# Three F blocks instead of two per step in the six-expert part of an attention and mixture-of-experts kernel: 15 block products for 18, sums kept in PSUM, prepared weights kept in DRAM

## The chip, the cores and the metric

The kernel runs on one core of one Trainium2 chip. The metric is the device time of one execution in microseconds (us), the median of several runs. Engines are named as in the profile: PE is the matrix engine (PEld its weight loads), DVE the vector engine, ACT the scalar engine, POOL the GpSimd engine, SP the engine that issues nearly all DMAs.

## The reference, cut to what matters

An attention-like recurrence over 768 positions (4 batches, 8 heads, head size 48) gives x, a matrix of N = 3072 tokens by D = 384. A mixture of experts follows:

```python
N, D, E, F = (3072, 384, 8, 1024)
logits = x @ w_gate
logits = logits - logits.max()
P = np.exp(logits)
for _ in range(8):
    P /= P.sum(1, keepdims=True) + 1e-09
    P /= P.sum(0, keepdims=True) + 1e-09
    P *= N / E
out = np.zeros((N, D), dtype=np.float32)
for e in range(E):
    h = np.maximum(x @ w1[e], 0.0)
    ye = h @ w2[e]
    out += P[:, e:e + 1] * ye
```

Every expert sees every token. Arithmetic is kept near fp32 by splitting each operand into a rounded high part and a low rest (`fp32r` tiles); a product is three matmuls, high by high, high by low, low by high.

## The kernel before

Three stages follow each other on PE. In phase 1 (`phase1`) the recurrence runs sub-block by sub-block of 256 tokens, and experts 0 and 1 run right behind it on the same tokens (`experts`); x is written to DRAM (`x_d`) and so are the two experts' results (`ye_d`). Phase 2a (`phase2a`) finishes experts 0 and 1 for the last sub-block, does the first three of the eight normalising rounds (`rows`, `columns`) and prepares the first tokens and weights. Phase 2b (`phase2b`) is the six-expert part: experts 2 to 7 for all tokens, and the other five rounds in its first steps.

The six-expert part takes the tokens in units of 768, each as two halves of 384 (`TH`), and F in blocks of 128. The first layer of one step multiplies 2 blocks of F (rows of a small block matrix A) by 3 blocks of D by the 2 token halves (blocks B11 to B32), which would be 12 block products of 128 x 128 by 128 x 384. It does them in 11, over sums of weight blocks (S1 to S5) and of token blocks (T1 to T4), in seven calls of `prod` (P1 to P7, four of them with two block products). Each `prod` fills a PSUM bank of its own from the pool `psA` of two; DVE and ACT combine them in SBUF tiles (`u2`, `u3`, `c11`, ...). `relu` makes the split activations `hh` and `hl` of each (F block, token half): one ACT and one DVE instruction.

The second layer of a step runs one step later: `second(st, k)` adds into the accumulator `po[k]`, one of six (3 token tiles by 2 halves, each a PSUM bank), 2 F blocks by 3 matmuls. `l2(k)` puts one such call behind each product, so PE alternates between the layers. There are 96 steps: 2 passes of tokens (`SU`), 6 experts, 2 units, 4 pairs of F blocks.

`prep_w` makes the weights of one pair: five sums on DVE, then four split pairs, the high part by ACT, the low part by DVE. It runs 48 times, since each pass prepares all weights anew from the raw weights, which `raw_w` loads. `load_x` makes the nine token blocks of a unit. When an expert is done, each accumulator is scaled by P and added to the output tile `oa` by DVE (L863).

PE runs in the order in which the program is written (`manual_schedule`). The instructions of ACT, DVE, POOL and SP are put in order by a scheduler, which moves weight and token preparation ahead to where it expects its data; each engine then runs its queue strictly in that order.

## Time and profile before

| what | value |
|---|---|
| runs | 1823.38, 1823.28, 1821.69 us; median 1823.28 us |
| profiled execution, span first to last instruction | 1819.5 us (3.8 us less than the median of the runs, which also hold what lies around the span) |
| mean granted TensorE clock | 0.997 |
| PE, PEld, DVE, ACT, POOL busy | 97%, 95%, 75%, 40%, 5% of the span |
| six-expert part, first to last matmul's start | 639.95 to 1813.26 us |
| bytes moved by DMA | 132.86 MB, 73 GB/s in the mean |

No time of the profiled execution itself is given beside its span. A busy PE is not a PE at its peak: a matmul of 384 columns has a duration of 335 ns in the profile, but matmuls overlap, and the distance between the starts of two is what counts. DVE instructions that follow each other without a wait overlap a little too. Rows in groups show the mean duration of one instruction in ns behind the total in us.

### The profile page before, as it was taken

The numbers are of one execution on the slowest core, as the hardware profiler recorded it, in microseconds if no ns is written. First come the engines' busy times: TensorE is split into PE (matmuls) and PEld (weight loads), VectorE is DVE, ScalarE is ACT, GpSimd is POOL, SyncE is SP. The second block draws the span as 40 slices with busy tenths as digits, with TensorE's granted clock in tenths as the row PEclk, the third lists the DMA queues.
The fourth block names the chain that finished last, engine by engine and source line by source line (L and its number), as shares of the span: only waits on it lengthen the run. The fifth ranks groups of instructions, "written<-read, shape, count | busy, mean of one in ns | idle before, by whom it ended". The sixth has DMA issues, their size and how long they took to land.

```text
span 1819.5 us, 30778 instructions
## 1 busy us (share of the span) xinstructions
PE 1768.3 (97%) x12062; PEld 1726.9 (95%) x12062; DVE 1360.0 (75%) x3038; ACT 730.1 (40%) x1607; POOL 89.4 (5%) x168
## 2 busy tenths in 40 slices
PE   6999899999999999999999999999999999999998
PEld 4888899999999989999999999998999999999998
DVE  8898999898863778867675767587776767675754
ACT  7544444454543533334242434243433334342421
POOL 3100211111110000000000000000000000000000
PEclk9999999999999999999999999999999999999999
DMA  7433534443422421301020101232220101020100
GB/s 223 120 101 103 134 107 123 128 111 98 117 80 91 137 81 53 122 18 53 1 70 1 59 12 53 71 105 68 88 70 18 53 18 53 2 69 1 53 27 29
DMA packets 104506, 132.86 MB, mean 73 GB/s; under 512 B 9632, under 2 KB 82080, under 8 KB 104352
## 3 DMA queue, kind: packets, MB, share of 16 engines
q1 hardware_dynamic: 98944, 120.89, 21.9%
q0 software_dynamic: 4608, 9.52, 2.1%
q8 instruction: 97, 1.59, 0.4%
q14 instruction: 57, 0.47, 0.1%
q10 hardware_dynamic: 800, 0.39, 0.1%
HBM read 88.22 MB, written 23.59 MB: 61 GB/s over the span
## 4 chain that ended last, share of the span: by engine, by line
PE 81%; DVE 11%; DMA 3%; ACT 2%; issue 1%; SPq 1%; DVEq 0%; ACTq 0%
PE po L856 10%; PE po L854 10%; PE po L855 10%; PE P L893 9%; PE P L894 9%; PE P L895 9%; PE ph L222 9%; PE po L195 3%; PE po L197 3%; PE po L196 3%; PE sp L561 2%; PE y L578 2%; DMA raw<-in_w_dram 1%; PE U L554 1%; DVE c L903 1%
## 5 line engine op out<-in xcount | busy, mean ns | idle before, releaser
L856 PE MATMUL po<-wc,hl 128*128 128x384 f32 x1152 | 385.9, 335 | 3.2 <-DVE hl L915 3.2
L854 PE MATMUL po<-wc,hh 128*128 128x384 f32 x1152 | 385.5, 335 | 0.1
L855 PE MATMUL po<-wc,hh 128*128 128x384 f32 x1152 | 385.4, 335 | 0.0
L914 ACT ACTIVATE hh<-c 128x384 fp32r<-128x384 f32 x384 | 200.9, 524 | 324.6 <-DVE c L903 323.1
L915 DVE SCALAR_TENSOR_TENSOR hl<-c,hh 128x384 fp32r<-128x384 f32 x384 | 212.8, 555 | 66.5 <-ACT hh L914 58.5
L222 PE MATMUL ph<-xh,w 128*128 128x256 f32 x1152 | 225.9, 281 | 2.1 <-ACT xh L630 1.2
L856 PEld LDWEIGHTS po<-wc,hl 128*128 128x128 f32 x1152 | 216.5, 188 | 4.7 <-DVE hl L915 4.7
L854 PEld LDWEIGHTS po<-wc,hh 128*128 128x128 f32 x1152 | 216.4, 188 | 0.4 <-ACT hh L914 0.4
L855 PEld LDWEIGHTS po<-wc,hh 128*128 128x128 f32 x1152 | 216.5, 188 | 0.0
L908 ACT ACTIVATE s<-P 128x384 f32<-128x384 f32 x192 | 94.1, 490 | 273.3 <-PE P L895 273.2
L222 PEld LDWEIGHTS ph<-xh,w 128*128 128x128 f32 x1152 | 185.5, 189 | 3.1 <-ACT xh L630 1.8
L234 ACT ACTIVATE hh<-ph 128x256 fp32r<-128x256 f32 x192 | 73.3, 382 | 223.5 <-PE ph L222 223.1
L893 PE MATMUL P<-B,wa 128*128 128x384 f32 x480 | 160.9, 335 | 0.9 <-DVE c L903 0.7
L895 PE MATMUL P<-B,wa 128*128 128x384 f32 x480 | 160.6, 335 | 0.0
L894 PE MATMUL P<-B,wa 128*128 128x384 f32 x480 | 160.6, 335 | 0.0
L222 PE MATMUL ph<-xl,w 128*128 128x256 f32 x576 | 153.9, 282 | 2.0 <-DVE xl L631 2.0
L195 PE MATMUL po<-w,hh 128*128 128x384 f32 x384 | 140.6, 366 | 0.6 <-ACT yst L200 0.5
L197 PE MATMUL po<-w,hl 128*128 128x384 f32 x384 | 130.1, 339 | 2.6 <-DVE hl L236 2.6
L903 DVE TENSOR_TENSOR c<-P,u 128x384 f32<-128x384 f32 x192 | 106.7, 556 | 31.0 <-PE P L895 29.6
L903 DVE TENSOR_TENSOR u<-u,s 128x384 f32<-128x384 f32 x96 | 53.5, 558 | 101.8 <-ACT s L908 101.7
L196 PE MATMUL po<-w,hh 128*128 128x384 f32 x384 | 129.4, 337 | 0.0
L236 DVE TENSOR_TENSOR hl<-hf,hh 128x256 fp32r<-128x256 f32 x192 | 80.4, 421 | 45.9 <-ACT hf L235 43.8
(175 smaller groups left out, 3516.6 us busy)
## 6 DMA issues: line engine op xcount, KB each, us to landing
raw<-in_w_dram SPq DMA_DIRECT2D x48, 768.0 KB, 4.3
qs<-z POOLq DMA_DIRECT2D x144, 64.5 KB, 3.7
qk<-in_aqk_dram SPq DMA_DIRECT2D x12, 768.0 KB, 6.0
ks<-kh SPq DMA_DIRECT2D x144, 64.0 KB, 3.1
ye_d<-yst SPq DMA_DIRECT2D x48, 192.0 KB, 2.1
y<-ye_d SPq DMA_DIRECT2D x48, 192.0 KB, 2.4
z<-in_aqk_dram SPq DMA_DIRECT2D x11, 768.0 KB, 5.6
B<-x_d SPq DMA_DIRECT2D x40, 192.0 KB, 4.0
```

The costliest lines, as they stand in the source:

```text
L195: nc.tensor.matmul(po[k], hh[:, s], w2h, start=f == 0, stop=False)
L196: nc.tensor.matmul(po[k], hh[:, s], w2l, start=False, stop=False)
L197: nc.tensor.matmul(po[k], hl[:, s], w2h, start=False, stop=f == NF - 1)
L222: nc.tensor.matmul(ph, w[:, k, ct * 128:ct * 128 + 128], x[:, ct, :], start=q == 0, stop=q == len(terms) - 1)
L854: nc.tensor.matmul(po[k], hh[:, s], w2[:, 0, i], start=first, stop=False)
L855: nc.tensor.matmul(po[k], hh[:, s], w2[:, 1, i], start=False, stop=False)
L856: nc.tensor.matmul(po[k], hl[:, s], w2[:, 0, i], start=False, stop=last)
L893: nc.tensor.matmul(ps, t[:, 0, k], x[:, 0], start=first, stop=False)
L894: nc.tensor.matmul(ps, t[:, 0, k], x[:, 1], start=False, stop=False)
L895: nc.tensor.matmul(ps, t[:, 1, k], x[:, 0], start=False, stop=last)
L914: A.activation(hh, c, AF.Relu)
L915: V.scalar_tensor_tensor(hl, c, 0.0, hh.bitcast(F32), ALU.max, ALU.subtract)
```

## The change

One step now takes three blocks of F: 3 rows of A by 3 blocks of D by 2 token halves, 18 block products done in 15 (P1 to P15, each one block product of three matmuls). There are 64 steps: 4 units, 16 sets of three F blocks (`NT`; a set may span two experts). One unit is now one pass over all weights; odd units go through the sets backwards.

- **Sums in PSUM.** The products run in a fixed order over two banks (`psX`): X and P use bank a, Y, Z and V bank b. A bank is read by ACT or DVE after a product, and the next product adds into the same bank, so the matmul has to wait until that reader is done. DVE does 10 additions and 6 `hl` a step, ACT 5 copies and 6 `hh`.
- **Second layer.** `order` lists 18 units (6 accumulators by 3 F blocks, three matmuls each); `fill(k)` puts k of them behind a product. At the start of a pass 8 (`FRONT`) come first.
- **Weights.** `prep_w` makes a set once, in the first unit: 12 sums on POOL (3 of 256 columns, 9 of 128), then six split pairs on ACT and DVE into four ring tiles (wa, wb, wc, wd), each stored to DRAM (`wd`). Units 1 to 3 load them with `load_set`, four DMAs of 768 KB a step. The raw weights of a set are one tile of 1152 KB, and there is one such buffer, so the load of the next set waits until POOL, ACT and DVE have read this one. The ring has 10 tiles (12 before).
- **Tokens.** All 15 token forms of unit 0 are made in phase 2a (`forms0`); those of the others ahead of time, and kept in DRAM (`xf`). In the last step of a unit `swap` loads a form's successor as soon as its product is done. Four forms are copied DRAM to DRAM without arithmetic.
- Phase 1 keeps two of expert 1's weight tiles in another pool; scaling of the first expert's tile moves to ACT.

```diff
-RING = 12
+RING = 10
+TRI = 3
+NT = (E - 2) * NF // TRI
+FRONT = 8
...
+    def raw_w(self, t):
+        raw = self.raw = self.wr.tile([128, TRI, 2 * C], F32, tag="raw", name=f"raw{t}")
...
+    def load_set(self, t):
+        W = self.ring(t)
+        for q, nm in enumerate(("wa", "wb", "wc", "wd")):
+            self.nc.sync.dma_start(W[nm].bitcast(F32).rearrange("p a b c -> p (a b c)"), self.wd[t][:, q])
+
+    def prep_w(self, t):
...
+        s = self.wr.tile([128, 11, 128], F32, tag="sum", name=f"sum{t}")
+        def sums():
+            def tt(o, a, b, op=ALU.subtract):
+                G.tensor_tensor(o, a, b, op)
+
+            tt(s[:, 0:2], R[:, 1, 0:2], R[:, 2, 0:2])
+            tt(s[:, 2:4], R[:, 0:2, 0], R[:, 0, 1:2].broadcast_to(sh))
+            tt(s[:, 4:6], R[:, 0:2, 2], s[:, 0:2])
...
+        def part(nm, k, src):
...
+            jobs.append(lambda: A.activation(o[0], src, AF.Copy))
+            jobs.append(lambda: V.tensor_tensor(o[1], src, o[0].bitcast(F32), ALU.subtract))
+        jobs.append(sums)
+        part("wc", slice(0, 5), R[:, 0, 1:6])
+        part("wc", 5, R[:, 1, 0])
+        store("wc")
+        part("wb", 5, R[:, 1, 2])
+        part("wa", slice(0, 6), s[:, 0:6])
+        store("wa")
+        part("wb", slice(0, 5), s[:, 6:11])
+        store("wb")
+        part("wd", None, R[:, 1:3, 3:6])
+        store("wd")
+        if t + 1 < NT:
+            jobs.append(lambda: self.raw_w(t + 1))
...
+        psA = c2.enter_context(tc.tile_pool(name="psX", bufs=1, space=PS))
...
+            def prod(nm, b, start, stop):
+                if start:
+                    pool, tag = (self.psC, {"Z": "po0", "P": "po1", "V": "po2"}[b]) if n == 0 and b in "ZPV" else (psA, "a" if b in "XP" else "b")
+                    bank[b] = pool.tile([128, TH], F32, tag=tag, name=f"{b}_{n}")
...
+                nc.tensor.matmul(ps, w[:, 0, k], x[:, 0], start=start, stop=False, skip_group_check=True)
+                nc.tensor.matmul(ps, w[:, 0, k], x[:, 1], start=False, stop=False, skip_group_check=True)
+                nc.tensor.matmul(ps, w[:, 1, k], x[:, 0], start=False, stop=True, skip_group_check=True)
+                if m == NT - 1 and u + 1 < NU:
+                    self.swap(u + 1, nm)
...
+            X = prod("P1", "X", True, False)
+            x1 = copy("x1", X)
+            fill(1)
+            Y = prod("P2", "Y", True, False)
+            c11 = copy("c11", Y)
+            fill(1)
+            prod("P4", "X", False, False)
+            add(c11, c11, X)
+            fill(1)
...
+            prod("P12", "X", False, True)
+            relu(1, 1, X)
+            fill(1)
+            prod("P5", "Z", False, True)
+            add(c11, c11, Z)
+            relu(0, 0, c11)
+            fill(1)
+            P = prod("P6", "P", True, True)
+            add(c21, c21, P)
+            relu(1, 0, c21)
+            fill(1)
+            V_ = prod("P15", "V", True, False)
+            add(c32, c32, V_)
+            relu(2, 1, c32)
+            fill(2)
...
+            prod("P14", "V", False, True)
+            add(c31, c31, V_)
+            relu(2, 0, c31)
+            fill(len(units))
```

Three places show how the queues change. A row reads line, instruction, output<-inputs, shape; numbers in a name are step or set, then a serial number.

**PE, between two products.** Before, the end of P4 and the start of P3 in step 21, each product in a bank of its own:

```order
L893 MATMUL P4_21_11497<-B31_1_8819,wa9_10673 128x384
L894 MATMUL P4_21_11497<-B31_1_8819,wa9_10673 128x384
L895 MATMUL P4_21_11497<-B31_1_8819,wa9_10673 128x384
L854 MATMUL po4_1_4_11510<-wc8_10539,hh01_20_11410 128x384
L855 MATMUL po4_1_4_11510<-wc8_10539,hh01_20_11410 128x384
L856 MATMUL po4_1_4_11510<-wc8_10539,hl01_20_11411 128x384
L854 MATMUL po4_1_4_11510<-wc8_10539,hh11_20_11366 128x384
L855 MATMUL po4_1_4_11510<-wc8_10539,hh11_20_11366 128x384
L856 MATMUL po4_1_4_11510<-wc8_10539,hl11_20_11367 128x384
L893 MATMUL P3_21_11517<-B22_1_8818,wb9_10674 128x384
L894 MATMUL P3_21_11517<-B22_1_8818,wb9_10674 128x384
L895 MATMUL P3_21_11517<-B22_1_8818,wb9_10674 128x384
```

After, P15 and P14 of step 8, which share the tile V:

```order
L1045 MATMUL V_8_10517<-xP15_0_8227,wb8_8_10161 128x384
L1046 MATMUL V_8_10517<-xP15_0_8227,wb8_8_10161 128x384
L1047 MATMUL V_8_10517<-xP15_0_8227,wb8_8_10161 128x384
L995 MATMUL po4_0_2_10140<-wc7_7_9956,hh00_7_10296 128x384
L996 MATMUL po4_0_2_10140<-wc7_7_9956,hh00_7_10296 128x384
L997 MATMUL po4_0_2_10140<-wc7_7_9956,hl00_7_10297 128x384
L995 MATMUL po4_0_2_10140<-wd7_7_9957,hh10_7_10309 128x384
L996 MATMUL po4_0_2_10140<-wd7_7_9957,hh10_7_10309 128x384
L997 MATMUL po4_0_2_10140<-wd7_7_9957,hl10_7_10310 128x384
L1045 MATMUL V_8_10517<-xP14_0_8226,wb8_8_10161 128x384
L1046 MATMUL V_8_10517<-xP14_0_8226,wb8_8_10161 128x384
L1047 MATMUL V_8_10517<-xP14_0_8226,wb8_8_10161 128x384
```

The number of second-layer matmuls between the two products is the same, six, but the second product now adds into the bank that the first one filled.

**ACT, where weights are split.** Before, from the first copy of step 14 to the first of step 15; wa9, wb9 and wc9 are the weights of pair 9, raw9 its raw tile:

```order
L908 ACTIVATE s1_14_10566<-P1_14_10562 128x384
L776 ACTIVATE wa9_10673<-raw9_10553 128x384
L776 ACTIVATE wa9_10673<-raw9_10553 128x256
L908 ACTIVATE s5_14_10599<-P5_14_10592 128x384
L776 ACTIVATE wb9_10674<-sum9_10672 128x640
L914 ACTIVATE hh11_14_10620<-c22_14_10603 128x384
L914 ACTIVATE hh00_14_10624<-c11_14_10618 128x384
L776 ACTIVATE wc9_10675<-raw9_10553 128x768
L914 ACTIVATE hh10_14_10643<-c21_14_10641 128x384
L914 ACTIVATE hh01_14_10662<-c12_14_10660 128x384
L908 ACTIVATE s1_15_10702<-P1_15_10698 128x384
```

After, the second half of step 9 up to the first copy of step 10, with the weights of set 11; sum11 is what POOL makes:

```order
L1063 ACTIVATE hh11_9_10684<-X_9_10558 128x384
L886 ACTIVATE wc11_11_10751<-raw11_10746 128x640
L886 ACTIVATE wc11_11_10751<-raw11_10746 128x128
L1063 ACTIVATE hh00_9_10697<-c11_9_10586 128x384
L1063 ACTIVATE hh10_9_10710<-c21_9_10616 128x384
L886 ACTIVATE wb11_11_10750<-raw11_10746 128x128
L1063 ACTIVATE hh21_9_10723<-c32_9_10628 128x384
L886 ACTIVATE wb11_11_10750<-sum11_10753 128x640
L886 ACTIVATE wa11_11_10749<-sum11_10753 128x768
L886 ACTIVATE wd11_11_10752<-raw11_10746 128x768
L1054 ACTIVATE x1_10_10761<-X_10_10757 128x384
L1063 ACTIVATE hh20_9_10739<-c31_9_10607 128x384
```

The whole of a set is now split inside one step, ahead of the copy x1 of the next step in the queue.

**SP, between two raw weight loads.** Before, five loads of raw weights stand one behind the other in the queue:

```order
L756 DMA raw9_10553<-in_w_dram 128x2x768
L756 DMA raw10_10689<-in_w_dram 128x2x768
L756 DMA raw11_10825<-in_w_dram 128x2x768
L756 DMA raw12_10967<-in_w_dram 128x2x768
L756 DMA raw13_11554<-in_w_dram 128x2x768
```

After, set 10's stores stand ahead of the load of set 11's raw weights:

```order
L844 DMA raw10_10545<-in_w_dram 128x768
L891 DMA wd10_153<-wc10_10_10552 128x1536
L891 DMA wd10_153<-wb10_10_10551 128x1536
L891 DMA wd10_153<-wa10_10_10550 128x1536
L891 DMA wd10_153<-wd10_10_10553 128x1536
L844 DMA raw11_10746<-in_w_dram 128x3x768
```

Four stores of 768 KB each now lie between two loads.

More of the change, by code (lines that the diff above doesn't have):

```diff
@@ new lines, in forms, with blk, job, add @@
+    def forms(self, u, pool, block, temp, dst, done):
+        nc, V, A = self.nc, self.nc.vector, self.nc.scalar
+        jobs = []
+        b = {}
+        def blk(c, j):
+            def job():
+                o = b[c, j] = block(c, j)
+                lo = temp()
+                for t, a in ((o, 0), (lo, 1)):
+                    nc.sync.dma_start(t.rearrange("p (s t) -> p s t", t=CH), self.x_d[u][:, :, a, c, j, :])
+                b["lo", c, j] = lo
+            def add():
+                V.tensor_tensor(b[c, j], b[c, j], b.pop(("lo", c, j)), ALU.add)
+            jobs.append(job)
+            jobs.append(add)
+        def summ(key, x, y, op):
+            def job():
+                if key not in b:
+                    b[key] = temp()
+                V.tensor_tensor(b[key], b[x], b[y], op)
+            jobs.append(job)
+        def split(nm, key, last=False):
+            t = {}
+            def hi():
+                t[0] = dst(nm)
+                A.activation(t[0][:, 0], b[key], AF.Copy)
+            def lo():
+                V.tensor_tensor(t[0][:, 1], b[key], t[0][:, 0].bitcast(F32), ALU.subtract)
+                done(nm, t[0])
+                if last:
+                    b.pop(key)
+            jobs.append(hi)
+            jobs.append(lo)
+        add, sub = ALU.add, ALU.subtract
+        B11, B12, B21, B22, B31, B32 = ((c, j) for c in range(3) for j in range(2))
+        blk(*B12)
+        blk(*B22)
+        summ("s", B12, B22, add)
+        split("P1", "s", True)
+        blk(*B11)
+        blk(*B31)
+        summ("t", B31, B11, sub)
+        split("P2", "t", True)
+        blk(*B21)
+        summ("d", B22, B21, sub)
+        split("P11", "d")
+        summ("d", "d", B12, add)
+        split("P4", "d")
+        summ("d", B11, "d", sub)
+        split("P3", "d", True)
+        blk(*B32)
+        summ("e", B32, B31, sub)
+        split("P14", "e")
+        summ("e", "e", B11, add)
+        split("P10", "e")
+        summ("e", "e", B12, sub)
+        split("P8", "e", True)
+        summ("f", B21, B31, add)
+        split("P6", "f", True)
+        summ("g", B22, B32, add)
+        split("P12", "g", True)
+        summ("h", B21, B32, add)
+        split("P13", "h", True)
+        return jobs
@@ L800, in more @@
                 self.moe.send(todo.pop(0))
-        for job in self.load_x(xa, 0, 0):
+        for job in self.forms0():
             job()
@@ L916, in relu @@
                 h[i, j] = (hh, hl)
-            def l2(k):
-                if prev is not None:
-                    second(prev, k)
-                if p > 1 or n == 0 or su and e == 2:
-                    for _ in range(min(2, len(jobs))):
-                        jobs.pop(0)()
-                if k == 1 and 0 < n <= ITERS - it:
-                    self.rows()
-                if k == 4 and 0 < n <= ITERS - it:
-                    self.columns(self.psA.tile([128, E], F32, tag="ph", name=f"cp{it + n - 1}"))
@@ new lines, in phase2b @@
+            if u and m == 0:
+                for _ in range(FRONT):
+                    unit(*units.pop(0))
+            X = prod("P1", "X", True, False)
[7 more added lines that the diff above has]
+            fill(1)
+            prod("P10", "Y", False, False)
+            c31 = copy("c31", Y)
+            fill(1)
@@ L943, in phase2b @@
             relu(1, 0, c21)
[L944 to L956 removed]
+            fill(1)
@@ new lines, in phase2b @@
+            V_ = prod("P15", "V", True, False)
+            add(c32, c32, V_)
+            relu(2, 1, c32)
+            fill(2)
+            if 0 < n <= ITERS - it:
+                self.columns(psA.tile([128, E], F32, tag="a", name=f"cp{it + n - 1}"))
+            prod("P14", "V", False, True)
+            add(c31, c31, V_)
+            relu(2, 0, c31)
+            fill(len(units))
+            while m == NT - 2 and xjobs:
+                xjobs.pop(0)()
+        last = steps[-1]
+        for k in range(2 * NS):
+            for i in range(TRI):
+                unit(last, k, i)
```

341 lines of the change are left out of this document (184 added, 157 removed).

## The prediction

> **What bounds the kernel now.** I read the page first (engine shares and the chain that ended last), then sums over stretches of the span, then the timeline of one steady step.
>
> ```profile
> span 1819.5 us, 30778 instructions
> PE 1768.3 (97%) x12062; PEld 1726.9 (95%) x12062; DVE 1360.0 (75%) x3038; ACT 730.1 (40%) x1607; POOL 89.4 (5%) x168
> ...
> PE 81%; DVE 11%; DMA 3%; ACT 2%; issue 1%; SPq 1%; DVEq 0%; ACTq 0%
> ```
>
> PE is busy nearly all the time and holds 81% of the chain; DVE at 75% is the next engine. The stretches below are phase 2a (596 to 642 us) and four of the six-expert part. Behind the stretch and its length stand busy us (and instructions) of PE, PEld, DVE, ACT and POOL, then granted clock, DMA share and GB/s.
>
> ```profile
> 596.00:642.00 46.00, 43.58 (x300) 42.51 (x299) 33.90 (x105) 25.18 (x64) 0.00 (x0) 1.00 0.47 147
> 642.00:740.00 98.00, 93.13 (x519) 90.31 (x517) 78.67 (x186) 35.01 (x71) 0.00 (x0) 0.98 0.23 69
> 740.00:1180.00 440.00, 438.00 (x2519) 436.30 (x2519) 302.67 (x626) 153.42 (x293) 0.00 (x0) 1.00 0.14 44
> 1180.00:1250.00 70.00, 64.94 (x367) 62.95 (x365) 57.60 (x124) 28.05 (x54) 0.00 (x0) 1.00 0.36 113
> 1250.00:1800.00 550.00, 546.74 (x3145) 544.90 (x3146) 377.82 (x774) 191.79 (x367) 0.00 (x0) 1.00 0.12 37
> ```
>
> ```profile
> 639.95 0.34 PE L893 MATMUL P<-B,wa 128*128 128x384 f32 x1
> ...
> 880.06 0.33 PE L893 MATMUL P<-B,wa 128*128 128x384 f32 x1
> ...
> 883.01 0.33 PE L895 MATMUL P<-B,wa 128*128 128x384 f32 x1
> ...
> 883.18 0.33 PE L854 MATMUL po<-wc,hh 128*128 128x384 f32 x1
> ...
> 883.38 0.56 DVE L903 TENSOR_TENSOR c<-P,u 128x384 f32<-128x384 f32 x1 [0.37 <-PE P L895]
> ...
> 1813.26 0.34 PE L856 MATMUL po<-wc,hl 128*128 128x384 f32 x1
> ```
>
> Between the starts at 880.06 and 883.18 us lie 18 matmuls of both layers: 3.12 / 18 = 0.1733 us each. That beat, not the 0.33 us duration, is the price of a matmul. The part runs from 639.95 to 1813.60 us, 1173.7 us. It has 96 steps of 11 x 3 + 12 x 3 = 69 matmuls, 6624 in all, and 6624 x 0.1733 = 1148.0 us. So 25.7 us are waits. By stretches (length less instructions x 0.1733): 8.1 us in 642 to 740, 3.5 in 740 to 1180, 6.4 in 1180 to 1250, 5.0 in 1250 to 1800. The two costly stretches are those in which token blocks are prepared and DVE is 80% busy; in the quiet ones 8.5 us in 990, 0.9%, are lost at 69% DVE.
>
> **Matmuls.** After, 64 steps of 15 x 3 + 18 x 3 = 99 matmuls make 6336. 288 fewer, x 0.1733 = **-49.9 us**. Shapes stay 128 x 128 by 128 x 384, so the beat should stay. A step of PE work is 99 x 0.1733 = 17.16 us. All that follows decides how much of this is kept; the 25.7 us of old waits go (**-25.7**) and new ones come.
>
> **DVE and ACT in a step.** These rows price them.
>
> ```profile
> L915 DVE SCALAR_TENSOR_TENSOR hl<-c,hh 128x384 fp32r<-128x384 f32 x384 | 212.8, 555 | 66.5 <-ACT hh L914 58.5
> L914 ACT ACTIVATE hh<-c 128x384 fp32r<-128x384 f32 x384 | 200.9, 524 | 324.6 <-DVE c L903 323.1
> L908 ACT ACTIVATE s<-P 128x384 f32<-128x384 f32 x192 | 94.1, 490 | 273.3 <-PE P L895 273.2
> L903 DVE TENSOR_TENSOR u<-P,u 128x384 f32<-128x384 f32 x96 | 53.3, 555 | 30.8 <-PE P L895 29.6
> L863 DVE SCALAR_TENSOR_TENSOR oa<-po,P,oa 128x384 f32<-128x384 f32 x120 | 73.9, 616 | 16.2 <-PE po L856 16.1
> L842 DVE SCALAR_TENSOR_TENSOR oa<-y,P,oa 128x384 f32<-128x384 f32 x48 | 28.7, 616 | 0.0
> L777 DVE TENSOR_TENSOR wc<-raw,wc 128x768 fp32r<-128x768 f32 x48 | 46.0, 958 | 11.9 <-ACT wc L776 11.7
> L777 DVE TENSOR_TENSOR wb<-sum,wb 128x640 fp32r<-128x640 f32 x48 | 39.4, 821 | 0.1
> L774 DVE TENSOR_TENSOR sum<-raw 128x128 f32<-128x128 f32 x144 | 35.8, 287 | 41.7 <-DMA raw<-in_w_dram 41.7
> L776 ACT ACTIVATE wc<-raw 128x768 fp32r<-128x768 f32 x48 | 40.6, 846 | 36.8 <-PE P L895 24.8 <-PE po L856 9.9 <-PE po L197 2.0
> L776 ACT ACTIVATE wb<-sum 128x640 fp32r<-128x640 f32 x48 | 35.5, 739 | 22.3 <-DVE sum L774 14.2 <-PE P L895 7.4
> L164 POOL CAST w<-wr 128x256 fp32r<-128x256 f32 x7 | 3.5, 539 | 6.4 <-PE wd L172 3.7 <-DMA wr<-in_w_dram 2.6
> L135 POOL CAST w<-wr 128x768 fp32r<-128x768 f32 x2 | 2.6, 1316 | 23.6 <-DMA wr<-in_w_dram 23.6
> ```
>
> Passes 2 to 4 (48 steps): DVE has 16 x 0.555 = 8.9 us a step, plus per pass 30 scalings and 12 additions of stored results (42 x 0.616 / 16 = 1.6) and 28 token operations (28 x 0.555 / 16 = 1.0): 11.5 of 17.16 us, 67%, about as in the quiet stretches now. ACT has 5 x 0.49 + 6 x 0.524 = 5.6 us. At 0.9% the loss is 48 x 17.16 x 0.009 = **+7 us**.
>
> The shared banks add waits. Two places are tight. P14 starts 7 beats after P15's last matmul, 1.21 us; the reader ends 0.37 + 0.56 = 0.93 us after that matmul's start if DVE is free (the row at 883.38 starts 0.37 us after the one at 883.01). P6 starts 10 beats after P12's last matmul, 1.73 us, and hh and hl of P12's sum take 0.37 + 0.52 + 0.56 = 1.45 us. Some 0.28 us are left at either. Of the 70 further DVE operations of a pass, 4.4 a step, about 0.8 fall into the 3 us around the two and push a reader by 0.5 us, some 0.25 beyond the slack. I take 0.2 a step, 48 x 0.2 = **+10 us**; the ends are 0 and one whole operation, 48 x 0.56 = 27 us.
>
> At the three ends of a unit 15 forms of 384 KB (5.9 MB) are loaded behind their products.
>
> ```profile
> q1 hardware_dynamic: 98944, 120.89, 21.9%
> ...
> raw<-in_w_dram SPq DMA_DIRECT2D x48, 768.0 KB, 4.3
> ...
> DMA to landing us min/median/max: 4.0/4.3/6.9
> ```
>
> 120.89 MB in 21.9% of the span is 303 GB/s with all DMA engines at work, so 5.9 MB take 19.5 us against a step plus eight units, 17.16 + 4.2 us. It fits barely. Between 0 and what the token stretch costs now (6.4 us), I take 2 us each: **+6 us**. The loads of 3.1 MB of weights a step take 10.4 us of 17.16 and are issued a step ahead: nothing, unless the queue stands.
>
> **The first pass, where the doubt lies.** One raw buffer makes weight preparation a ring: the last DVE split of a set, the raw load of the next, POOL's sums, ACT's splits, the last DVE split again. In ACT's queue all of a set stands ahead of the copy x1 of the next step, and P4 waits for that copy, so a step cannot be shorter than the ring. Its links:
>
> - Raw load, 1152 KB: 4.3 x 1.5 = 6.5 us alone; with all four stores of 768 KB ahead (2.6 us each at 303 GB/s) up to 6.5 + 10.4 less some 4 that have drained, 13. I take one full store ahead, 9, since the others are issued earlier; 0.4 us for the issue.
> - POOL's sums: 9 of 128 columns, 3 of 256. No stretch of the six-expert part shows POOL at work (x0 above), and no row shows it adding. Low end, DVE's price: 9 x 0.287 + 3 x 0.42 = 3.8 us. The casts give (1316 - 539) / 512 = 1.52 ns a column, 0.345 for 128, hence 9 x 0.345 + 3 x 0.539 = 4.7 us with one input; twice that, 9.4, is the high end. I take 6.
> - ACT's wb, wa, wd behind the sums: 0.739 + 0.846 + 0.846 = 2.4; DVE's wd 0.96.
>
> Together 0.4 + 9 + 6 + 2.4 + 1.0 = 18.8 us, 1.7 over PE's 17.16; the ends are 14.1 (hidden) and 26.2 us. For 14 steps **+24 us**. DVE says about the same: 8.9 + 4.1 for splits (2 x 0.958 + 2 x 0.821 + 2 x 0.287) + 2.7 of the rest, 15.7 of 17.16 us, 91%; at 80% the stretch 642 to 740 lost 8.1 on 90 us, 9%, or 1.5 us a step. Both end at the same copy, so I count the longer, not their sum.
>
> [...]
>
> **Phase 2a.** DVE gets 17 more token operations (28 for 11), 9.4 us on 33.9 busy of 46. The two sets prepared there cost DVE 8.2 us, the two pairs before 8.4 (their sums go to POOL). Set 2's split stands in ACT's queue ahead of step 0's x1 and needs a raw load behind set 1's stores and POOL's sums, up to 12 us late. Between 0 and 12 I take **+6 us**. The end behind the last matmul stays; 24 small DRAM copies go into SP's queue in phase 1 and 2a, where it waits between sub-blocks: nothing, 3 us if a load of the next sub-block slips behind them.
>
> **Sum.** -49.9 - 25.7 + 7 + 10 + 6 + 24 + 6 = -22.6, hence a span of 1797. The profile's span lies 3.8 us under the median of the runs (1823.28), so 1801 us, 1.2% less; 0.2% (3.6 us) is about what a measurement can tell from no change.
>
> **Rivals.**
>
> *Preparation hides.* Ring below 17.16 us (POOL at 4.7 and the load at 8 give 16.5) and phase 2a for nothing: 1801 - 24 - 6 = 1771. For it: preparing weights now costs PE little, 0.9% in the quiet stretches. Against: DVE at 91%.
>
> *The first pass is bound by its ring, slower than before.* It decides where 14 steps lose 22.6 us more than the 24 of the sum, 3.3 us each over PE's step: a ring of 20.5 us. POOL at 9.4 with the load at 10 gives 23.2, 6.0 a step, 84 in all: 1801 - 24 + 84 = 1861. [...]
>
> *The two banks cost every step one DVE operation.* 27 for 10 in passes 2 to 4 and 9 more in the first: 1801 + 26 = 1827. For it: 0.28 us of slack. Against: now, too, PE takes back a bank of `psA` soon, at 0.9% loss.
>
> **Chances.** Forecast (1780 to 1820) 0.43; hidden 0.20; ring-bound 0.22; banks 0.11; rest 0.04. Faster by over 0.2%: 0.42 + 0.20 + 0.05 + 0.02 = 0.69; slower: 0.20 + 0.04 + 0.02 = 0.26; same 0.05. The range runs from the hidden case, 1770, into the ring-bound one, 1850, and leaves out 0.18.
>
> **What the changed profile would show.** 6336 matmuls at a beat of 0.173 in the six-expert part; in passes 2 to 4 steps of 17.3 to 17.6 us; in the first pass steps near 19, with ACT's wb or wa waiting for POOL and wc for the raw load; POOL's twelve sums near 6 us a set. The forecast is wrong if the first pass's steps are at 17.2 or beyond 21, if PE waits for DVE at P14 in every step, or if products wait for DMA.

## The result and the profile after

The changed kernel takes 1834.97 us (median of 4 runs, 1833.08 to 1842.75) against 1823.33 of the kernel before in the same comparison (1821.69 to 1826.55): ratio 1.008, interval 1.0053 to 1.0106. It is slower, where 1801 and "faster" were forecast. The profiled execution has a span of 1841.0 us; it is the longest of the four runs (the spans of the others lie between 1831.3 and 1834.4), so some 7 to 10 us of what is lost below belong to that run.

The page's head and chain:

```profile
span 1841.0 us, 31212 instructions
PE 1747.9 (95%) x11774; PEld 1691.1 (92%) x11774; DVE 1283.5 (70%) x2710; ACT 745.6 (41%) x1673; POOL 209.0 (11%) x360
...
PE 72%; DVE 14%; DMA 7%; issue 2%; ACT 2%; POOL 2%; SPq 1%; DVEq 0%; ACTq 0%; POOLq 0%
```

12062 - 11774 = 288 matmuls are gone, as forecast; DVE has 328 instructions fewer. But PE's share of the chain fell from 81% to 72%, and DMA's rose from 3% to 7%: PE waits more. Where, sums over stretches show (columns as in the prediction: length; busy us and instructions of PE, PEld, DVE, ACT, POOL; granted clock; DMA share; GB/s). They are phase 2a, the first pass, ten microseconds inside phase 2a, and a quiet stretch of pass 2.

```profile
596.00:659.10 63.10, 52.02 (x368) 50.31 (x368) 44.82 (x115) 30.24 (x76) 15.90 (x25) 0.92 0.72 244
659.10:984.50 325.40, 289.59 (x1566) 274.70 (x1566) 252.03 (x467) 142.64 (x288) 103.53 (x167) 0.98 0.70 255
648.10:658.30 10.20, 4.93 (x16) 4.93 (x17) 7.10 (x22) 1.51 (x4) 0.88 (x2) 0.50 0.98 343
1001.00:1119.00 118.00, 118.00 (x683) 118.00 (x683) 62.78 (x120) 41.65 (x84) 0.00 (x0) 1.00 0.52 182
```

In the quiet stretch PE is never idle: 118.00 / 683 = 0.1728 us a matmul, and a step of 99 takes 17.16 us. There the change does all that it was priced at. The time is lost elsewhere. Against the beat of 0.1733 us, with matmuls counted in the program, the six-expert part (now 659.10 to 1835.15 us) holds 1176.0 - 1098.0 = 78 us of waits, for 25.7 before:

| stretch | lost, us |
|---|---|
| phase 1: PE starts its thousandth matmul at 152.2 instead of 144.2, and stays that late up to phase 2a | 8.0 |
| phase 2a: the first product starts at 659.10 instead of 639.95, 19.2 us late | 11.2 more |
| step 0: 19.6 us for 45 matmuls (7.8) | 11.8 |
| steps 1 to 14: 284.5 us, 20.3 a step, for 14 x 17.16 | 44.3 |
| steps 24 to 28, in pass 2 | 12.9 |
| changes of unit: first steps of units 1 to 3 (steps 16, 32, 48), 2.4 each | 7.1 |
| all other steps | 2 |

Check: -49.9 (matmuls) + 78 - 25.7 + 19.2 = +21.6, and 1841.0 - 1819.5 = 21.5. The first pass (steps 0 to 14) alone loses 56 us, more than the matmuls gain.

The 8.0 us of phase 1 are for the most part this run's own. The profile of the kernel before grants the full clock throughout its first 150 us. Here half the clock was granted for 3.41 us from 37.1 us and for 6.83 us each from 91.7 and 125.8, and PE waited 2.6 us once at 34. The kernels of the experiments below are 2.1 to 7.3 us late at the same matmul; whether the 2 us that all of them have come from the change is not shown.

**The ring in the first pass.** A set's way is a loop: the last DVE split frees the one raw buffer, the next raw load fills it, POOL makes the sums, and ACT and DVE split again. These are rows from the timelines of four engines of the changed kernel from 703 to 727 us, cut to set 4 (start, duration; in brackets the idle time before and what ended it). DVE's last split of a set, for sets 3 and 4:

```profile
704.20 0.95 DVE L887 TENSOR_TENSOR wd<-raw,wd 128x768 fp32r<-128x768 f32 x1
...
723.23 0.94 DVE L887 TENSOR_TENSOR wd<-raw,wd 128x768 fp32r<-128x768 f32 x1
```

SP's issues of the raw loads of sets 4 and 5:

```profile
705.59 1.33 SPq L844 DMA_DIRECT2D raw<-in_w_dram  x1
...
724.62 1.82 SPq L844 DMA_DIRECT2D raw<-in_w_dram  x2
```

POOL's sums of set 4, the first six and the last:

```profile
714.42 3.75 POOL L868 TENSOR_TENSOR sum<-raw 128x256 f32<-128x256 f32 x6 [16.46 <-DMA raw<-in_w_dram]
...
721.50 0.46 POOL L868 TENSOR_TENSOR sum<-sum 128x128 f32<-128x128 f32 x1
```

ACT's last splits of set 4, and x1 of the next step behind them:

```profile
720.42 0.85 ACT L886 ACTIVATE wa<-sum 128x768 fp32r<-128x768 f32 x1 [0.80 <-POOL sum L868]
721.17 0.83 ACT L886 ACTIVATE wd<-raw 128x768 fp32r<-128x768 f32 x1
721.91 0.47 ACT L1054 ACTIVATE x<-X 128x384 f32<-128x384 f32 x1
```

The last split of a set ends at 705.15; 0.44 us later the raw load is issued; POOL starts 8.8 us after that, when the block is there; its sums take 7.5 us to 721.96; ACT, which already stood waiting for them, splits wa and wd, and only then copies x1 for the next step; DVE splits wd to 724.17, and the next load is issued. 705.15 to 724.17 is 19.0 us, and no link has slack: each starts when the one before ends or when its engine gets to it (in the 1.2 us between ACT's split of wd and DVE's, DVE splits wa and does a small reduction). Over sets 4 to 15 the ring takes 20.3 us in the mean (705.15 to 949.0, 12 sets): the length of a step. As one set is made per step, the two lengths agree whichever holds up the other; what shows that the ring counts are the experiments.

PE's own waits in the first pass (what waits, for what: us in total, times, longest):

```profile
PE V L1045 <- DVE c L1058: 12.0, 11, 2.6
PE X L1045 <- ACT x L1054: 7.2, 4, 5.0
PE X L1045 <- DVE c L1058: 5.1, 7, 1.3
PE Y L1045 <- DVE c L1058: 4.8, 7, 1.5
PE P L1045 <- DVE hl L1064: 3.3, 3, 1.5
```

PE stands for ACT's x1 in step 0 (5.0 us) and for some 2 us after it. In steps 1 to 14 it is held up mostly by DVE's additions at the banks, V first (9.4 us in 10 waits there).

### The profile page after: what moved, and what is told of

Same layout as the page of the kernel before. It is cut to its first block, busy times and chain, and to the rows that moved or that the text cites. A ratio compares the mean times of both kernels' runs of the same rounds, so it can differ in the third digit from the quotient of the medians.

```text
span 1841.0 us, 31212 instructions
## 1 busy us (share of the span) xinstructions
PE 1747.9 (95%) x11774; PEld 1691.1 (92%) x11774; DVE 1283.5 (70%) x2710; ACT 745.6 (41%) x1673; POOL 209.0 (11%) x360
## 4 chain that ended last, share of the span: by engine, by line
PE 72%; DVE 14%; DMA 7%; issue 2%; ACT 2%; POOL 2%; SPq 1%; DVEq 0%; ACTq 0%; POOLq 0%
PE po L997 9%; PE po L995 9%; PE po L996 9%; PE ph L232 8%; PE po L205 3%; PE X L1045 3%; PE X L1047 3%; PE X L1046 3%; DMA raw<-in_w_dram 3%; PE po L207 3%; PE po L206 3%; PE Y L1045 2%; PE Y L1047 2%; PE Y L1046 2%; PE sp L572 2%
## 5 line engine op out<-in xcount | busy, mean ns | idle before, releaser
L1058 DVE TENSOR_TENSOR c<-c,X 128x384 f32<-128x384 f32 x192 | 105.9, 552 | 231.9 <-PE X L1047 190.0
L997 PE MATMUL po<-wd,hl 128*128 128x384 f32 x768 | 257.7, 336 | 0.0
L995 PE MATMUL po<-wd,hh 128*128 128x384 f32 x768 | 257.5, 335 | 0.0
L996 PE MATMUL po<-wd,hh 128*128 128x384 f32 x768 | 257.5, 335 | 0.0
L1063 ACT ACTIVATE hh<-c 128x384 fp32r<-128x384 f32 x256 | 134.0, 524 | 188.9 <-DVE c L1058 188.6
L1054 ACT ACTIVATE c<-Y 128x384 f32<-128x384 f32 x192 | 94.2, 491 | 156.3 <-PE Y L1047 156.0
L995 PEld LDWEIGHTS po<-wd,hh 128*128 128x128 f32 x768 | 144.9, 189 | 0.0
L997 PEld LDWEIGHTS po<-wd,hl 128*128 128x128 f32 x768 | 144.7, 188 | 0.3 <-DVE hl L1064 0.3
L996 PEld LDWEIGHTS po<-wd,hh 128*128 128x128 f32 x768 | 144.8, 189 | 0.0
L996 PE MATMUL po<-wc,hh 128*128 128x384 f32 x384 | 129.2, 336 | 0.0
L995 PE MATMUL po<-wc,hh 128*128 128x384 f32 x384 | 129.1, 336 | 0.0
L997 PE MATMUL po<-wc,hl 128*128 128x384 f32 x384 | 129.1, 336 | 0.0
L534 POOL DMA_DIRECT2D qs<-z x144 | 77.1, 542 | 443.0 <-issue 114.3
```

The costliest lines, as they stand in the source:

```text
L995: nc.tensor.matmul(po[k], hh[:, s], w2[0], start=c == 1, stop=False)
L996: nc.tensor.matmul(po[k], hh[:, s], w2[1], start=False, stop=False)
L997: nc.tensor.matmul(po[k], hl[:, s], w2[0], start=False, stop=c == NF)
L1054: A.activation(o, a, AF.Copy)
L1058: V.tensor_tensor(o, a, b, ALU.add)
L1063: A.activation(hh, c, AF.Relu)
```

## Experiments

Each kernel was compared with the kernel before on the same chip. "Steps 1-14" and "24-28" are what these steps of the profiled execution take beyond 17.16 us each; the kernels are in the order of the text.

| kernel | median, us | ratio to before, interval | first product at | steps 1-14 | 24-28 |
|---|---|---|---|---|---|
| changed kernel | 1835.0 | 1.008, 1.0053-1.0106 | 659.1 | +44.3 | +12.9 |
| no_sums | 1809.0 | 0.9927, 0.9911-0.9944 | 651.4 | +18.4 | +10.7 |
| wd_first | 1831.6 | 1.0057, 1.0038-1.0075 | 661.8 | +35.6 | +10.1 |
| pace | 1838.3 | 1.0088, 1.0073-1.0103 | 655.9 | +48.0 | +6.1 |
| head_two | 1844.6 | 1.0118, 1.0099-1.0137 | 649.4 | +52.5 | +10.6 |
| no_load | 1824.4 | 1.0018, 1.0006-1.0031 | 659.4 | +31.4 | +7.8 |
| slack | 1834.0 | 1.0069, 1.0052-1.0086 | 652.1 | +45.0 | +6.9 |
| dve_sums | 1840.6 | 1.0099, 1.0077-1.0121 | 655.1 | +46.0 | +9.9 |
| y_own_pace | 1850.9 | 1.0152, 1.0131-1.0172 | 658.4 | +49.4 | +7.5 |
| forms_pool | 1831.5 | 1.006, 1.0047-1.0074 | 645.7 | +48.2 | +2.6 |
| forms_pool_wd | 1828.4 | 1.0046, 1.0031-1.0061 | 653.1 | +38.5 | +2.2 |
| eleven_tiles | 1836.2 | 1.0091, 1.0077-1.0104 | 655.4 | +44.0 | +8.1 |
| sums_late | 1834.0 | 1.0062, 1.0044-1.008 | 661.1 | +37.1 | +8.5 |
| sums_late_pool | 1823.1 | 1.0007, 0.9995-1.0018 | 654.7 | +35.0 | +1.8 |
| sums_late_pool_23 | 1826.9 | 1.0021, 1.0009-1.0033 | 655.1 | +37.1 | +3.1 |
| sums_mid | 1820.3 | 0.9986, 0.9977-0.9995 | 659.0 | +24.4 | +8.9 |
| sums_mid_pool | 1817.5 | 0.9975, 0.9964-0.9986 | 657.5 | +29.2 | +1.9 |
| mid_pool_slack | 1808.4 | 0.9922, 0.991-0.9934 | 654.6 | +21.1 | +2.6 |
| mid_slack | 1814.1 | 0.9952, 0.9939-0.9965 | 659.4 | +24.1 | +6.8 |

Kernels that leave phase 2a as it was in the program still start their first product anywhere from 652 to 659 us; where nothing there was touched, steps 24 to 28 lose 7 to 13 us, and steps 1 to 14 from 44.0 to 49.4. Differences of that size in one profile show nothing, and the changed kernel's profile is of a run 8 us above its median. Phase 1 holds 2.1 to 8.0 us of what the first product is late; phase 2a itself is longer than before by 3.0 us in forms_pool, 4.3 in head_two and 8.5 to 15.8 in the others. Verdicts go by the medians and intervals first. The medians of the kernel before lie between 1821.4 and 1823.5 in these comparisons, and two kernels are told apart only where the intervals of their ratios do not touch. Where an edit is shown, it is cut to its main lines (`...`).

### Is it the ring, or DVE?

**no_sums** leaves out POOL's sums and splits the raw blocks in their place.

```
-        jobs.append(sums)
...
-        part("wa", slice(0, 6), s[:, 0:6])
+        part("wa", slice(0, 6), R[:, 1, 0:6])
...
-        part("wb", slice(0, 5), s[:, 6:11])
+        part("wb", slice(0, 5), R[:, 2, 0:5])
```

> Leaves out POOL's twelve sums: wa and wb are split straight from raw, so that the weights are not the needed ones; all else stays. Theory R (the first pass is bound by its ring: raw load 8.9 us, POOL's sums 7.3, ACT's and DVE's last splits 4.1, together the 20.3 us that a step of the first pass takes): the ring falls to about 14 us, below PE's 17.16, the first pass goes from 325 us to 275-285 and the run to about 1790. Theory D (DVE, 77% busy there and slowed by POOL, holds PE up, with or without the ring): only what POOL takes from DVE comes back, some 1.2 us a step, 1815. Theory Q (the loads and stores of the first pass hold PE up): no change, 1835.

Sums over steps 1 to 14, first of the changed kernel:

```profile
678.65:963.16 284.51, 257.23 (x1397) 244.59 (x1397) 229.65 (x425) 129.06 (x261) 98.51 (x156) 0.98 0.69 251
```

And of no_sums:

```profile
672.48:931.13 258.65, 249.59 (x1398) 241.36 (x1398) 206.85 (x421) 128.60 (x259) 0.00 (x0) 1.00 0.74 274
```

26 us less in the median (34 between the profiled runs, 26 of them in these steps); R had said 45, D 20. The sums are the largest single item, but not all of it. DVE needs 22.8 us less (229.65 and 206.85) for 425 and 421 instructions; some 2 us are the four more that fall into the longer stretch, so POOL at work had cost it about 1.5 us a step.

**wd_first**: wd, which needs no sum, is split ahead of wa and wb and kept there in the queues of ACT and DVE (`issue_after`, not shown), and the next raw load goes out behind its store.

```
+        part("wd", None, R[:, 1:3, 3:6])
+        store("wd")
+        if t + 1 < NT: jobs.append(lambda: self.raw_w(t + 1))
         part("wa", slice(0, 6), s[:, 0:6])
...
```

> The same work in another order: wd, which needs no sum, is split ahead of wa and wb, and the next raw load is issued behind wd's store, ahead of the stores of wa and wb. ACT's and DVE's last splits thus leave the ring: issue and load 8.9 us, POOL's sums 7.3, together 16.2 us. Theory R: steps of the first pass at 17.2 to 18, about 35 to 45 us less, 1795. Theory D: the same work on DVE and POOL, within 0.3% of 1835.

3.4 us, and the intervals overlap: nearly nothing. The ring's floor fell only to some 18.7 us: the tile that wd of set n+2 takes is wb of set n, which P14 still reads, so the split, and with it the raw load, stays at the end of the step.

**no_load** leaves out the raw loads of sets 2 to 15.

```
-        if t + 1 < NT:
+        if t + 1 < 2:
             jobs.append(lambda: self.raw_w(t + 1))
```

> Leaves out the raw loads of sets 2 to 15: all of them are prepared from set 1's raw block, so that the stored weights are not the needed ones. The instructions on PE, DVE, ACT and POOL stay, and so does their order. Theory R (ring): without the 8.9 us of load the ring is 11.5 us, below PE's step; steps 2 to 14 go from 20.1 to 17.2-17.6, the run to about 1795. Theory D (DVE's queue: 14.4 us of work a step and 1.4 more that POOL's sums cost it, with splits ahead of the additions that free a bank): the same queue, 1825-1835. Theory Q (DMA traffic of the first pass): 1.15 MB a step fewer, as R.

10.5 us less: R had said 40. POOL's waits in steps 1 to 14 tell why:

```profile
POOL sum L868 <- DVE wa L887: 129.5, 11, 15.4
```

Without a load to wait for, POOL waits for DVE's split that frees the one tile of sums. There is a second loop behind the first, and the splits still stand in a row at the step's end, ahead of x1 on ACT and of the addition after P4 on DVE.

**dve_sums**

```
-                G.tensor_tensor(o, a, b, op)
+                V.tensor_tensor(o, a, b, op)
```

> The twelve sums of a set on DVE instead of POOL. They take 3.9 us there by the rows of the kernel before, so DVE has 14.4 + 3.9 = 18.3 us a step of the first pass, 1.1 over PE's 17.16, and POOL no longer slows it. Theory D: steps of 18.5 to 20.5, as many or more waits as now, 1825-1850. Theory R: the ring falls to 8.9 + 3.9 + 4.1 = 16.9 us, steps of 17.2 to 17.6, 1795.

Steps 1 to 14 of dve_sums:

```profile
677.47:963.67 286.20, 258.45 (x1397) 243.66 (x1397) 241.96 (x577) 128.56 (x259) 0.00 (x0) 0.99 0.67 248
```

DVE works 242 of 286 us, 17.3 a step, more than PE's 17.16, and the time is as D forecast. But DVE is idle for 15% of the stretch, and the loop has not become shorter: load with its issue 9.3 us, sums 5.4 and some 6 more up to the last split, 20.6 in the mean of the same twelve sets, where R had 16.9. The links stand in DVE's fuller queue. So R's 1795 is out, and which of the two bounds this kernel is not told by it.

**forms_pool**: the three operations of `forms` (28 a unit) go to POOL.

```
-                V.tensor_tensor(b[c, j], b[c, j], b.pop(("lo", c, j)), ALU.add)
+                nc.gpsimd.tensor_tensor(b[c, j], b[c, j], b.pop(("lo", c, j)), ALU.add)
...
```

> All additions and subtractions that make the forms of the tokens (28 a unit) go from DVE to POOL, at 0.55 us each 15 us for every unit; the preparation of weights stays as it is. Theory D (in the first pass a step is as long as DVE's work there over 0.81, 16.4 / 0.81 = 20.3): steps 1 to 14 carry some 14 such operations, 8 us of DVE, so the first pass loses 10 us, phase 2a some 8 of its 19, and steps 24 to 28, where DVE stands for a load of a token block, 10 of their 12.6: 1808-1815. Rival R (ring): POOL's sums come later behind the token operations in its queue, the ring is longer, 1840 or more. Rival C (POOL slows DVE for as long as it saves): 1835.

Steps 1 to 14 of forms_pool:

```profile
670.99:959.46 288.47, 256.83 (x1398) 243.24 (x1398) 220.78 (x383) 129.41 (x262) 145.05 (x198) 0.99 0.69 248
```

9 us less work on DVE in steps 1 to 14, and they are no shorter (4 us longer in this profile); the run is 3.4 us shorter in the median, with intervals that overlap, where D had 20 or more: D falls for the changed kernel. The first product starts 13 us earlier, 8 of them won in phase 2a, but step 0 is 5.7 us longer. Steps 24 to 28 are down from 12.9 to 2.6. **forms_pool_wd** adds wd_first:

> forms_pool and wd_first together. If the two add up (wd_first alone gave -3.4 us against the changed kernel): forms_pool less 3 to 8 us, 1800-1812. If the ring is what forms_pool makes longer, wd_first takes more off here than alone, 8 us or over.

Another 3 us in the median, as much as wd_first alone, again with intervals that overlap; the run stays above the forecast.

### Side theories

**slack**: units of the second layer are moved within the step (`fill`): P15 to P14 gets 9 matmuls for 6, and P12 to P6 12 for 9.

```
...
             relu(2, 1, c32)
-            fill(2)
+            fill(3)
```

> Second-layer units are moved within the step: three instead of two between P15 and P14, two instead of one behind P12, one instead of two behind P11 and behind P3. P14 comes 9 matmuls behind P15 where it was 6, P6 12 behind P12 where it was 9; P3 and P12 lose 3 and 6. Theory B (the first pass pays at the places where a bank's reader has little slack): the waits at V (10.8 us in steps 1 to 14) and P (4.1) nearly go, with the half clock behind them 12 to 18 us, the run at 1818-1823. Theory D (DVE is late by whole splits, and the wait is taken at the next bank): within 4 us of 1835.

No change: the waits at V stay (11.0 us in 13, for 9.4 in 10). While DVE is late by whole splits, more room at one place did not help.

**eleven_tiles**: one weight tile more, paid for with one buffer less for the token forms (`st`, 2 for 3) and one less for the copies c (`ct`, 8 for 9).

```
-RING = 10
+RING = 11
...
```

> Eleven weight tiles for ten, paid by two slots for three of the forms and eight for nine copies c. With ten, set n+2's wc takes over wa of set n and can be written only behind P12 of step n, and its wa and wb only behind the last units, so that the splits fall into the end of a step. Theory T (this clump makes the waits): with eleven the splits spread, V and X waits halve, 1820. Theory D (DVE's total decides): within 4 us of 1835; the scarcer slots may cost some.

No change; the tiles for split weights are not what holds the order by themselves, unless the two scarcer buffers cost as much as the tile gains.

**head_two**: two Sinkhorn iterations in phase 2a for three. The last iteration then comes after expert 3's first scalings, which use P of seven iterations.

> Two of the eight Sinkhorn iterations ahead of the first product where there were three, and six in the steps where there were five. Theory P (in phase 2a PE waits 8.4 us for the third iteration behind DVE's queue, and runs at half clock for 10 us after it; such waits add up): first product some 10 us earlier, 1825. Theory R (the ring of weight sets runs from phase 2a on, and set 2, not the first product, sets step 0 and all that follow): the first product is earlier, step 0 longer by as much, the run within 3 us of 1835.

Its first product is 9.7 us earlier (6.8 of them in phase 2a, the rest in phase 1), and the run is 9.6 us longer in the median, with intervals that just overlap: steps 0 and 1 take 50.1 us for 42.6, and the mean granted clock of the profiled execution is 0.984 for 0.986. P falls. The time won ahead of the ring was not kept; R, which had the run within 3 us of 1835, does not say why it became longer.

**pace** and **y_own_pace** hold the next unit's forms to their places in the program (`issue_after` on the last copy and addition); the second gives y a tile of its own.

> The token operations of the next unit are kept from running ahead: each may be issued only behind the copy and the addition that stand ahead of it in the program, so that a step has two or three of them where now steps 1, 12, 27 and 28 have up to eleven. Theory B (the clumps, with y and the forms in the same three slots, make steps 24 to 28 longer by 12.6 us): these steps go to 17.2-17.4 and the run to about 1823; in the first pass nothing, since its ring decides. Rival: those steps wait for loads of stored weights, which share the queue with y and the forms: no change, 1835.

> As pace, and the stored results y get a tile of their own, one expert's 192 KB at a time, instead of sharing three slots with the next unit's forms. Theory S (pace left steps 24 to 28 at 91.9 us for 85.8, and made 40 to 43 as slow, since the forms wait for slots that y holds): both go to 17.2-17.5 a step, 1825 to 1828. Rival (DVE waits in order for the loads of x_d's blocks, which are issued when the slot before is free): steps 25 to 28 stay at 18-19, 1838.

Both miss. pace halves the loss in steps 24 to 28 and loses 4 us in steps 41 to 43, which now have forms; y_own_pace is worse, since DVE waits in order for the loads of y (7.0 us, 4 times, in step 25 alone). S falls. The changed kernel's timeline shows DVE standing for a load, first on DVE:

```profile
1158.79 0.56 DVE L740 TENSOR_TENSOR xb<-xb,xt 128x384 f32<-128x384 f32 x1 [2.14 <-DMA xt<-x_d]
1159.27 0.55 DVE L1058 TENSOR_TENSOR c<-c,V 128x384 f32<-128x384 f32 x1
```

Then on PE:

```profile
1159.87 0.52 PE L1045 MATMUL Y<-xP,wc 128*128 128x384 f32 x1 [1.84 <-DMA wb<-wd]
```

The addition that frees bank b for P2 stands behind a token addition that waits for its block. (The profile names a load of wb as PE's releaser; that matmul reads wc, and it starts 0.05 us after that addition ends, at 1159.82.) forms_pool puts this wait on POOL, where no reader of a bank stands behind it, and the loss goes.

### The loops through the queues

**sums_late**: on top of wd_first, the two splits that read sums are queued behind the next step's copy c32 on ACT, and on DVE behind the last addition ahead of them in the program.

```
-                        st.enter_context(self.tc.issue_after(wd[i].ins))
+                        st.enter_context(self.tc.issue_after((self.la, self.lv)[i].ins if self.la else wd[i].ins))
...
```

> wd_first, and the two splits that read POOL's sums (wa, and 640 columns of wb) are queued on ACT and DVE behind the copies and additions of the next step that stand ahead of them in the program, where they were queued ahead of that step's first copy x1. The same instructions. Theory L (the loop runs through the queues: x1 stands behind splits that wait for POOL, P4 waits for x1, and at the step's end DVE has all splits in a row ahead of the additions that free a bank): steps 2 to 14 at 17.3 to 18.3, the first pass some 25 us shorter than now, 1800-1812. Theory D (DVE's total, 16 us a step over 0.81): 19.5 a step as in wd_first, 1830. Theory R (raw load, sums and wd's split, wherever the others stand): 8.8 + 7.4 + 2.7 = 18.9 a step, 1825.

POOL's waits from 690 to 950 us, of the changed kernel:

```profile
POOL sum L868 <- DMA raw<-in_w_dram: 183.3, 14, 25.5
```

And of sums_late:

```profile
POOL sum L870 <- DVE wb L898: 186.1, 13, 46.9
```

x1 waits for no sum any more, but now POOL waits for the tile of sums instead of the raw block, and since raw is freed by POOL's last sum, the load comes late too: 18.4 to 18.7 us in every quiet step, a loop again. At 1834.0 us L's 1800 to 1812 is out. **sums_late_pool** and **sums_late_pool_23**:

> sums_late and forms_pool together. Under L, what forms_pool lost in the first pass (POOL's sums behind token operations, and x1 behind both) is gone too, since x1 waits for no sum, and its gains in phase 2a (first product 13 us earlier) and in steps 24 to 28 (8 us) stay: 1780-1795. Under R the sums come later in POOL's queue: 1820-1828.

> As sums_late_pool, but the forms of unit 1, made in the first pass, stay on DVE; POOL makes those of unit 0 (phase 2a) and of units 2 and 3. Under L within 6 us of sums_late_pool, either way; under C (POOL's 1.1 us token operations, which read SBUF beside DVE, cost DVE as much as they save) 5 us or more faster than it.

Steps 2 to 4 are the same in all three (18.66, 18.40, 18.42; 18.62, 18.39, 18.42; 18.64, 18.39, 18.41), with DVE's work from 15.8 to 16.6 us a step: a loop of fixed length sets them, not DVE's total. Both medians are above what L forecast, and C falls: sums_late_pool_23 is not faster than sums_late_pool but 3.8 us slower.

**sums_mid**: the two splits earlier in the step, behind the copy c31 on ACT and behind the step's first addition (`lv0`) on DVE, so that the tile is free before the block lands. The edit is against sums_late.

```
-                self.la = A.activation(o, a, AF.Copy)
+                c = A.activation(o, a, AF.Copy)
+                if nm == "c31":
+                    self.la, self.lv = c, self.lv0
...
```

> As sums_late, but the two splits stand earlier in the step: on ACT behind the copy c31 (the third) where it was c32 (the fifth), on DVE behind the first addition. In sums_late POOL waited 186 us in 13 sets for DVE's split of wb, which frees the one tile of sums (L870 <- DVE wb L898), and the raw load waited for POOL's last sum: a loop of 8 to 9 us of load, 7.7 of sums and the wait between, 18.6 us, which every quiet step showed (18.39 to 18.66). Theory F (that loop is the floor of the quiet steps): with the tile free before the raw block lands the floor falls to about 17.2 (8.8 + 7.4 = 16.2 is below PE's step), 13 steps by 1.2 us, 1815-1820. Rival (PE waits at Y and P for DVE whatever POOL does): 18.6 stays, 1832.

POOL's waits from 690 to 950 us, the two longest groups:

```profile
POOL sum L870 <- DMA raw<-in_w_dram: 113.5, 9, 16.5
POOL sum L870 <- DVE wb L898: 10.7, 1, 10.7
```

And steps 1 to 14:

```profile
677.10:941.71 264.61, 250.61 (x1397) 240.21 (x1397) 224.17 (x425) 129.01 (x261) 94.30 (x156) 1.00 0.74 272
```

POOL waits for the block again and, but for one set, no longer for the tile, and the run is 13.6 us shorter than sums_late, about F's 13 x 1.2. With the same instructions, the order of the splits, the raw load and the stores alone took the changed kernel from 1835.0 to 1820.3, from slower than before to faster by 0.14% (the interval leaves out 1). **sums_mid_pool**:

> sums_mid and forms_pool together. By F the same 13 to 16 us less than sums_late_pool (1823), 1806-1812, below the kernel before; by the rival 1823.

1817.5: 14 us better than forms_pool, and 2.8 better than sums_mid in the median, where the intervals overlap; 5 to 12 us above the forecast.

**mid_pool_slack**, **mid_slack**: the units of slack on top of both.

> sums_mid_pool with the units of slack (three between P15 and P14). What is left in its steps 1 to 14 (29.2 us) is led by V's place, 9.8 us in 12 steps, of 0.4 to 1.6 us each. Theory B (six matmuls between P15 and P14 are too few for a DVE that also splits weights): now that DVE is no longer late by whole splits, 0.52 us more of room takes half or more of them, 4 to 8 us, 1809-1814. Theory D (the wait goes to the next bank, as in slack alone): within 3 us of 1817.5.

> sums_mid with the units of slack: the same question without forms_pool. Theory B: V's 8.6 us halved, 1812-1816. Theory D: within 3 us of 1820.

Now the room counts, 9.1 and 6.2 us in the medians, and the intervals do not touch; in the changed kernel the same edit gave nothing. With sums_mid_pool it takes the waits at V from 8.0 to 3.7 us; without forms_pool V's waits do not shrink in the profile (7.1 and 8.0), so where those 6.2 us come from is not shown. mid_pool_slack, 1808.4 us, beats the changed kernel and the one before: 0.8% under the kernel before, 1.4% under the changed one. Its steps 1 to 14:

```profile
676.18:937.54 261.36, 252.99 (x1397) 241.34 (x1397) 221.51 (x384) 128.38 (x263) 140.95 (x195) 0.99 0.75 275
```

It still loses 21 us in steps 1 to 14, with DVE at 221.5 of 261.4 us, 85%. Much the same share stands in sums_mid (85%) and dve_sums (85%). That DVE bounds the rest is likely but was not tried.

## Why the prediction was wrong, by its steps

The forecast was wrong in direction. Its span, 1797, is 44 us under the profiled 1841. The measured 1835 lies between the 1770 and 1850 that it allowed only because these reached into the ring-bound case. The 3.8 us that it added from span to run were too many, too: the changed kernel's runs exceed their spans by 1.8 to 1.9.

**Matmuls, -49.9, and old waits, -25.7.** Right: 288 fewer at an unchanged beat.

**Quiet loss +7 and shared banks +10.** The quiet steps lose nothing: 17.16 us, though DVE reads each shared bank with 0.28 us of slack. 0.28 us is enough while DVE is busy 53% of the time (62.78 of 118.00). Passes 2 to 4 lose 15 us all the same, nearly all of it in five steps and for another cause: the prediction named the loads as a matter of PE ("products wait for DMA") and not of DVE, which waits in its queue with a bank's reader behind it. The rival of the two banks did not come true in these passes; in the first pass the banks are where a late DVE is felt (9.4 us at V in steps 1 to 14).

**Ends of units, +6.** 7.1, for another reason: the loads stay hidden. The eight units put ahead of P1 are missing at the end of that step, where Z and V wait uncovered:

```profile
996.16 0.44 PE L1045 MATMUL Z<-xP,wb 128*128 128x384 f32 x1 [0.59 <-DVE c L1058]
999.21 0.45 PE L1045 MATMUL V<-xP,wb 128*128 128x384 f32 x1 [0.82 <-DVE c L1058]
```

**The first pass, +24.** The ring exists, but it was sized too small, and it was tied to PE at the wrong place. It was put at 18.8 us and measured 20.3 for 14 steps, +44.3 us. The links: load with its issue 9.4 forecast, 9.1 measured (8.2 to 10.3 in twelve sets); POOL's sums 6 forecast, 7.5 measured; the splits behind them 3.4 forecast, 2.2 in the ring shown and 3.7 in the mean, from 0.8 to 7.6, since ACT and DVE have other work in their queues. With 20.3 in place of 18.8 the forecast would have been 1821, no gain. The rival "bound by its ring" got 0.22 and decides from 20.5 us: the ring came out just short of that, and the terms of phase 2a made up the rest.

Two steps of the working failed. POOL's sums were priced without what DVE does to them (below): that term, 6 for 7.5, is the whole difference of the ring. And "both end at the same copy, so I count the longer, not their sum" is wrong: in steps 1 to 14 PE waits some 2 us for that copy, x1, and 24 for DVE, whose additions stand behind the splits. Ring and DVE hold each other up, since the links stand in the queues of ACT and DVE behind other work. The runs show that neither alone gives the time: in the medians, 10.5 us go without the loads, 26 without the sums, and 3.4, within the noise, with DVE relieved of the tokens.

**Phase 2a, +6.** The 6 us stood for set 2's split ahead of x1 in ACT's queue. That wait came, in step 0, which lost 11.8 us, 5.0 of them at P4 for x1. What the sum put at nothing is PE's own place behind DVE's longer queue in phase 2a, 11.2 us. PE's waits in phase 2a are led by

```profile
PE cp L720 <- DVE cs L716: 9.5, 2, 8.3
```

From 642 us up to the third iteration's `cs`, 8.3 us of token operations and splits go through DVE's queue, and PE stands for 8.3 us. Within that wait, at 648.1 us, the clock falls to half for 10.2 us (the stretch from 648.10 above); the 16 matmuls in it take 4.9 us where the beat gives at most 2.8. Together that is most of the 11.2. The other 8.0 us that the first product is late come from phase 1, which the forecast left as it was, and mostly from this one run.

**POOL and DVE.** Both take longer while the other works, and POOL's sums came to 7.5 us a set, between the 6 of the sum and the 9.4 of the ring-bound rival. At the shortest POOL adds 128 columns in 0.45 us; the means of its groups of such additions lie between 0.56 and 0.64. Its operations beside DVE, from its timeline:

```profile
719.14 0.77 POOL L868 TENSOR_TENSOR sum<-sum,raw 128x128 f32<-128x128 f32 x1
719.87 0.51 POOL L868 TENSOR_TENSOR sum<-sum 128x128 f32<-128x128 f32 x1
...
721.50 0.46 POOL L868 TENSOR_TENSOR sum<-sum 128x128 f32<-128x128 f32 x1
```

And DVE's `hl` at that time:

```profile
717.82 0.77 DVE L1064 SCALAR_TENSOR_TENSOR hl<-c,hh 128x384 fp32r<-128x384 f32 x1
718.98 0.61 DVE L1064 SCALAR_TENSOR_TENSOR hl<-c,hh 128x384 fp32r<-128x384 f32 x1
720.06 0.74 DVE L1064 SCALAR_TENSOR_TENSOR hl<-c,hh 128x384 fp32r<-128x384 f32 x1
```

`hl` takes 0.55 us alone and 0.61 to 0.77 here; over steps 1 to 14 those that read c take 0.66 in the mean, and 0.55 in no_sums. DVE's additions that read a bank do not change (0.55 in both). At the shortest durations of the trace, 0.45 us for 128 columns and 0.72 for 256, a set's sums would take 9 x 0.45 + 3 x 0.72 = 6.2 us. So both engines pay (about 1.5 us a step on DVE, 1.3 on POOL, 7.5 for 6.2), but for part of the time they work at once: beside the sums of set 4, DVE ran splits and `hl` that take 3.0 us alone, and 6.2 + 3.0 = 9.2 us of work took 7.5.

## What to carry to other kernels

When preparation runs beside the main work, draw every loop that a single buffer closes, through the in-order queues that its links stand in: an instruction that waited held up what stood behind it in its queue here (a token addition that stood 2.14 us for a load, the addition behind it that frees bank b), and the order of the splits, a load and the stores was worth 15 us, more than the change was slower by. A late reader on a busy engine made a shared bank cost time here (9.4 us at V in steps 1 to 14), and room at the bank paid (9.1 and 6.2 us) only once the reader was no longer late by whole splits, so test such edits again after each fix. Terms that end at the same place may be counted by the longer only if they share no queue.
